# Two heads of 48 on partitions 0-47 and 64-111: attention products in parts of the TensorE array instead of zero-padded ones

## The chip, the core and the metric

The kernel runs on one core of one Trainium2 chip. A core has a matrix engine (TensorE, PE in the profile; its weight loads are PEld), a vector engine (VectorE, DVE), a scalar engine (ScalarE, ACT), GpSimd (POOL) and a queue engine (SyncE, SP) that here only issues DMAs. Each engine works through its own list of instructions in order and waits on semaphores. The metric is the device time in microseconds, lower is better. Matrix products write to PSUM, which VectorE and ScalarE read; everything else lies in SBUF, with 128 partitions.

## What is computed

A recurrent attention with a decaying state per head, then two matrix products with a squared ReLU between. Shapes: 4 batches, 8 heads, 768 tokens, head size 48; the second part has 3072 tokens, width 384, hidden width 2048. All is float32 in value (the weights of the second part come as float64).

```python
def _attn_ref(r, k, v, w, u):
    B, H, S, D = r.shape
    state = np.zeros((B, H, D, D), dtype=np.float32)
    y = np.zeros_like(r)
    for t in range(S):
        kt, vt, rt, wt = (k[:, :, t], v[:, :, t], r[:, :, t], w[:, :, t])
        cur = np.einsum('bhd,bhe->bhde', u[None] * kt, vt)
        y[:, :, t] = np.einsum('bhd,bhde->bhe', rt, state + cur)
        state = wt[:, :, :, None] * state + np.einsum('bhd,bhe->bhde', kt, vt)
    return y.astype(np.float32)

def _moe_ref(x, w_in, w_out):
    h = np.maximum(x @ w_in, 0.0)
    return (h * h @ w_out).astype(np.float32)
```

## The kernel before

Tokens are cut into 6 chunks of 128 (c), and a unit is one chunk of one batch (b), all 8 heads: 24 units. Within a chunk the recurrence becomes products of matrices: scores of the scaled keys and queries under a causal mask, their product with the values, and the product of the queries with the state before the chunk. Heads are worked on in four pairs; the 48 + 48 rows of a pair lie on partitions 0 to 95.

A unit passes through these stages:

- `load` and `load_v` (lines 129 to 141) bring w, k, r and v with tokens on partitions. v goes into a tile in which each head is followed by 48 zero columns.
- `spread` (line 143) brings w, r and k to head dimensions on partitions. In chunk 0 TensorE transposes them; later VectorE transposes blocks of 32 by 32 into z (line 160) and 12 DMAs (line 164) put the blocks into pt. It also keeps the running maximum of a test on w (`far`, line 169) and makes `beta`, the diagonal of the scores.
- `decay` (line 183): VectorE's scans over w (line 192), ScalarE's logarithm and exponential, and the scaled queries pt[:, 1] and keys pt[:, 2]. To keep a pair's heads apart in a 96-row product, zeros stand in place of the other head: in the keys in chunks 0 and 1 (Kz), and from chunk CR = 2 on in the queries, split into a leading float32r part and the rest (Rh, Rl, Kh, Kl; lines 218 to 227). Em is the decay over the chunk, laid out as a block diagonal.
- `ktok` (line 234): TensorE transposes the keys back (ktp, four products).
- `scores` (line 244), in two halves of four heads: products into mt, then a masked copy by VectorE onto M (line 257), which ScalarE has filled with beta on the diagonal (line 249). In chunks 0 and 1 four float32 products make a half; later six float32r products of 256 columns.
- `mix` (line 261): for each pair one product with the state (line 269, from chunk 1 on) and two with M and the zero-padded values (line 272) into yb. ScalarE and VectorE split yb into two float32r parts (lines 278, 279). Three pairs go straight into xT; the fourth goes through x3 and three DMAs (line 281) into xT's partitions 96 to 127.
- `state` (line 283): dS from keys and values (line 289), added to the batch's state S and scaled by Em.

The second part takes a chunk's four batches together. `moe_h` makes 128 hidden columns for 512 tokens: 9 products hp, three for each third of the width (line 307); ScalarE, VectorE and GpSimd turn them into the squared ReLU, again in two parts. `moe_o` multiplies these with w_out: 12 products ob, three for each batch (line 322). A step is one hidden block f of 16, and ob runs LAG = 3 steps behind hp. In chunk 0 the first six steps are done for two batches at a time. Weights are loaded and split into float32r parts by `load_w` and `split_w`, the first NW blocks in one pool, the others in the place of chunk 0's tiles.

The program is written in the order of a table of positions: each stage of a unit has an offset in steps (STAGES, STAGES0, lines 333 to 340), units follow each other every four steps, and everything is sorted by position. From that, the framework's scheduler sets each engine's list at build time by its own estimate of when things are ready. On the chip this list is fixed. The PSUM pool `ps_a`, two buffers of one bank, serves ktp, mt, yb and dS.

```python
    AFTER = [(decay, 2, state), (spread, 2, mix), (load_v, 2, state), (load, 2, spread)]
    ...
                x = (4 + 6 * b if c == 1 else 8 * (i - B)) + off
    ...
        at_pos(x + 0.01, half_h, c, f, bs)
        at_pos(x + n / 2 + 0.01, put, LAG)
```

A last part (from line 431) does everything again token by token if a decay was too small; with these inputs it isn't run.

Of the kernel before, what the change touches and what calls it, by code (L numbers as in the profile page):

```python
# [22 lines left out]
def kernel(  # L23
# [16 lines left out]
    C = 128  # L40
    NC = S // C
    NP = H // 2
    R = 2 * D
    NF = DF // 128
    KT = DM // 128

    NW = 11
    CR = 2
# [14 lines left out]
    far = const.tile([128, H * D], F32, name="far")  # L63
    V.memset(far, 0.0)
    nmid = const.tile([128, 1], F32, name="nmid")
    G.memset(nmid, -W_MID)
    blk = at.tile([R, 2, D], F32, name="blk")
    G.memset(blk, 1.0)
    G.affine_select(out=blk[:, 0], in_=blk[:, 0], pattern=[[0, D]], compare_op=ALU.is_ge,
                    fill=0.0, base=D - 1, channel_multiplier=-1)  # L70
    G.affine_select(out=blk[:, 1], in_=blk[:, 1], pattern=[[0, D]], compare_op=ALU.is_ge,
                    fill=0.0, base=-D, channel_multiplier=1)
# [6 lines left out]
    zero = at.tile([R, 1], F32, name="zero")  # L79
# [5 lines left out]
    decays = at.tile([R, NP, C + 1], F32, name="decays")  # L85
    V.memset(decays[:, :, 0:1], 1.0)
    Vps = [at.tile([128, H, 2, D], F32, name=f"Vp{i}") for i in range(2)]
    for t in Vps:
        V.memset(t, 0.0)
    Ss = [at.tile([R, NP, R], F32, name=f"S{b}") for b in range(B)]  # L90

    # Weights come as the bits of float64; a block of them gives way to its float32r parts, the
    # leading one and the rest, which take its place.
# [4 lines left out]
    def load_w(f):  # L98
# [5 lines left out]
        for ps, src in ((slice(0, R), w_in32[f, 0:KT * R]), (slice(R, 128), w_in32[f, KT * R:])):  # L104
            nc.sync.dma_start(out=ri[ps], in_=src.rearrange("(k p) x -> p k x", k=KT))
# [20 lines left out]
    # One unit: the C tokens of chunk c in batch b, all heads; its stages pass tiles on in `un_`.  # L126
    un_ = {}

    def load(c, b):
        ss = slice(c * C, c * C + C)  # L130
        st = ld.tile([128, 3, H * D], F32, name="st")
        for i, src in ((0, w), (2, k), (1, r)):
            nc.sync.dma_start(out=st[:, i].rearrange("s (h d) -> s h d", d=D),  # L133
                              in_=src[b, :, ss, :].rearrange("h s d -> s h d"))
        un_[c, b] = {"st": st}

    def load_v(c, b):
        ss = slice(c * C, c * C + C)
        vp = Vps[(c * B + b) % 2]
        nc.sync.dma_start(out=vp[:, :, 0], in_=v[b, :, ss, :].rearrange("h s d -> s h d"))  # L140
        un_[c, b]["vp"] = vp
# [372 lines left out]
```

## Time and profile before

| | us |
|---|---|
| median of 3 runs | 620.69 |
| lowest and highest run | 620.52, 625.94 |
| profiled execution: span of its instructions | 621.0 |
| TensorE matmuls busy | 557.3 (90%) |
| TensorE weight loads busy (beside the matmuls) | 506.8 (82%) |
| VectorE busy | 414.7 (67%) |
| ScalarE busy | 315.8 (51%) |
| GpSimd busy | 267.1 (43%) |

The profiled execution gives no other time of its own than this span.

The profile is of one execution. A row of a timeline begins with its start and its length in us, then engine, source line, operation, the tiles written and read, shape and count; in brackets the idle time of the engine ahead of it, and what ended it. Lengths of matmuls are modelled and overlap, so a rate is read from start to start. A table of stretches gives busy time and count for each engine, then the clock granted to TensorE as a share of its full speed, then the share of the DMA engines and GB/s.

### The profile page before, as it was taken

The numbers are of one execution on the slowest core, as the hardware profiler recorded it, in microseconds if no ns is written. First come the engines' busy times: TensorE is split into PE (matmuls) and PEld (weight loads), VectorE is DVE, ScalarE is ACT, GpSimd is POOL, SyncE is SP. The second block draws the span as 40 slices with busy tenths as digits, with TensorE's granted clock in tenths as the row PEclk, the third lists the DMA queues.
The fourth block names the chain that finished last, engine by engine and source line by source line (L and its number), as shares of the span: only waits on it lengthen the run. The fifth ranks groups of instructions, "written<-read, shape, count | busy, mean of one in ns | idle before, by whom it ended". The sixth has DMA issues, their size and how long they took to land.

```text
span 621.0 us, 9387 instructions
## 1 busy us (share of the span) xinstructions
PE 557.3 (90%) x3224; PEld 506.8 (82%) x3224; DVE 414.7 (67%) x639; ACT 315.8 (51%) x697; POOL 267.1 (43%) x228
## 2 busy tenths in 40 slices
PE   3476968798699998999999999999999999999994
PEld 2466958697497997988998999999989999988994
DVE  5789799887876857776967987686576765211110
ACT  3767556555565643554663655555366545242321
POOL 3364366523754534426444553353543332233230
PEclk9988779979899997999999999999999999999998
DMA  9976677257136543245445335424525230010001
GB/s 181 255 138 150 111 162 163 45 123 138 32 60 122 98 75 51 43 70 98 103 73 89 55 65 128 81 44 74 87 46 115 49 54 7 8 51 2 1 0 55
DMA packets 214212, 51.21 MB, mean 82 GB/s; under 512 B 198160, under 2 KB 212112, under 8 KB 214160
## 3 DMA queue, kind: packets, MB, share of 16 engines
q1 hardware_dynamic: 210704, 45.84, 39.5%
q10 hardware_dynamic: 3456, 4.72, 2.1%
q8 instruction: 27, 0.44, 0.3%
q14 instruction: 25, 0.20, 0.1%
HBM read 31.65 MB, written 4.72 MB: 59 GB/s over the span
## 4 chain that ended last, share of the span: by engine, by line
PE 61%; DVE 19%; DMA 5%; SPq 5%; issue 3%; POOL 3%; ACT 3%; DVEq 0%; ACTq 0%; POOLq 0%
PE hp L307 25%; PE ob L322 23%; PE yb L272 5%; PE mt L253 4%; DVE decays L192 3%; PE yb L269 2%; SPq L164 2%; DMA ri<-in_moe_w_in_dram 2%; DVE Rl L223 2%; DVE z L160 2%; SPq L133 2%; DVE q L116 2%; DVE t L311 1%; DVE pt L199 1%; DVE q L118 1%
## 5 line engine op out<-in xcount | busy, mean ns | idle before, releaser
L307 PE MATMUL hp<-xT,wi 128*128 128x512 f32 (+1 forms) x918 | 225.9, 391 | 16.2 <-DVE t L311 13.0
L314 POOL TENSOR_TENSOR g<-t,g 128x512 fp32r<-128x512 f32 (+1 forms) x102 | 134.2, 1317 | 235.6 <-ACT g L313 231.3
L322 PE MATMUL ob<-wo,g 128*128 128x384 f32 x1152 | 220.9, 340 | 0.0
L307 PEld LDWEIGHTS hp<-xT,wi 128*128 128x128 f32 x918 | 167.2, 193 | 48.5 <-DVE t L311 14.9
L322 PEld LDWEIGHTS ob<-wo,g 128*128 128x128 f32 x1152 | 201.8, 190 | 3.7
L311 DVE SCALAR_TENSOR_TENSOR t<-hp,t 128x512 f32<-128x512 f32 (+1 forms) x102 | 66.7, 654 | 123.3 <-ACT t L310 123.1
L313 ACT CAST g<-t 128x512 fp32r<-128x512 f32 (+1 forms) x102 | 60.4, 592 | 101.5 <-PE ob L322 53.6
L310 ACT ACTIVATE t<-hp 128x512 f32<-128x512 f32 (+1 forms) x102 | 57.9, 567 | 69.7 <-PE hp L307 65.8
L249 ACT ACTIVATE M<-ident,beta 128x128 f32<-128x128 f32 x192 | 64.3, 392 | 10.3 <-PE yb L272 7.2
L272 PE MATMUL yb<-M,Vp 128*96 128x128 f32 x384 | 60.0, 285 | 1.6 <-DVE M L257 1.5
L257 DVE COPY_PREDICATED M<-caus,mt 128x512 f32<-128x512 uint8 x48 | 35.2, 735 | 28.9 <-PE mt L253 22.1
L272 PEld LDWEIGHTS yb<-M,Vp 128*96 128x96 f32 x384 | 50.4, 174 | 2.2 <-DVE M L257 2.2
L173 POOL TENSOR_TENSOR st<-st 128x384 f32<-128x384 f32 x24 | 28.3, 1177 | 39.4 <-DVE z L160 38.0
L192 DVE TENSOR_TENSOR_SCAN decays<-pt,zero 96x128 f32<-96x128 f32 x80 | 41.1, 568 | 1.6 <-DMA pt<-z 1.5
L223 DVE SCALAR_TENSOR_TENSOR Rl<-pt,blk,Rh 96x512 fp32r<-96x512 f32 x32 | 34.4, 1087 | 0.2 <-ACT Rh L222 0.2
L269 PE MATMUL yb<-pt,S 96*96 96x128 f32 x160 | 31.0, 274 | 0.0
L174 POOL TENSOR_TENSOR st<-st,un 128x384 f32<-128x384 f32 x24 | 29.1, 1214 | 1.8
L160 DVE STREAM_TRANSPOSE z<-st 128x1152 f32<-128x1152 f32 x20 | 27.1, 1354 | 0.0
L240 PE MATMUL ktp<-ident,pt 96*128 96x96 f32 x80 | 11.2, 267 | 17.5 <-issue 7.9
L240 PEld LDWEIGHTS ktp<-ident,pt 96*128 96x128 f32 x80 | 9.2, 152 | 21.4 <-issue 9.1
L197 ACT ACTIVATE y<-decays 96x512 f32<-96x512 f32 x20 | 12.6, 630 | 27.0 <-DVE decays L192 26.9
L256 PE MATMUL mt<-pt,Kz 96*128 96x128 f32 x128 | 22.8, 338 | 2.7 <-DVE S L291 2.0
(79 smaller groups left out, 659.9 us busy)
## 6 DMA issues: line engine op xcount, KB each, us to landing
pt<-z SPq DMA_DIRECT2D x240, 48.0 KB, 2.1
ro<-in_moe_w_out_dram SPq DMA_DIRECT2D x16, 384.0 KB, 5.9
ri<-in_moe_w_in_dram SPq DMA_DIRECT2D x16, 288.0 KB, 5.7
st<-in_w_dram SPq DMA_DIRECT2D x24, 192.0 KB, 3.7
st<-in_k_dram SPq DMA_DIRECT2D x24, 192.0 KB, 4.1
st<-in_r_dram SPq DMA_DIRECT2D x24, 192.0 KB, 3.9
Vp<-in_v_dram SPq DMA_DIRECT2D x24, 192.0 KB, 3.5
out_dram<-os ACTq DMA_DIRECT2D x24, 192.0 KB, 1.9
```

What stands on the lines that cost most here:

```text
L160: V.transpose(out=z.rearrange("a q x i -> a x q i"), in_=st.rearrange("s t (p q x) -> s (t p) q x", q=3, x=32))
L192: V.tensor_tensor_scan(out=E[:, p, 1:C + 1], data0=wv[:, p], data1=zero.broadcast_to([R, C]), initial=1.0, op0=ALU.mult, op1=ALU.add)
L223: V.scalar_tensor_tensor(out=Rl[:, :, j], in0=Rt, scalar=blk[:, j, 0:1], in1=Rh[:, :, j].bitcast(F32), op0=ALU.mult, op1=ALU.subtract)
L249: A.activation(M[:, x], ident, AF.Copy, scale=d["beta"][:, 4 * q + x:4 * q + x + 1])
L269: T.matmul(yb[:, p], Ss[b][:, p], d["pt"][:, 1, p], start=True, stop=False)
L272: T.matmul(yb[:, p], vp[:, o:o + R], d["M", p // 2][:, 2 * (p % 2) + j], start=(c == 0 and j == 0), stop=(j == 1))
L307: T.matmul(hp, wi[f][:, wl, kt * 128:kt * 128 + 128], xT[:, kt, xl, xs], start=(m == 0), stop=(m == 3 * KT - 1))
L310: A.activation(t, hp, AF.Relu)
L311: V.scalar_tensor_tensor(out=t, in0=hp, scalar=0.0, in1=t, op0=ALU.max, op1=ALU.mult)
L313: A.copy(out=g[:, 0], in_=t)
L314: G.tensor_tensor(out=g[:, 1], in0=t, in1=g[:, 0].bitcast(F32), op=ALU.subtract)
L322: T.matmul(obs[b][:, 0:DM], g[:, gl, (b - bs[0]) * C:(b - bs[0]) * C + C], wo[f][:, wl], start=(f == 0 and n == 0), stop=(f == NF - 1 and ...
```

## The change

Each head of a pair gets 64 partitions: the even head lies on 0 to 47, the odd one on 64 to 111. Products then take one head at a time in a part of the array, by the partitions of their operands and their results:

- scores: 48 rows by 128 columns, one half of the array's rows for each head, 8 float32 products into two PSUM tiles, one per head parity. The float32r split from chunk 2 on is gone (Rh, Rl, Kh, Kl), and so are Kz and `blk`.
- yb: the state product takes a quarter of the array (48 rows, 64 or 48 columns), 8 of them instead of 4; the product with M takes half the columns, 8 as before, with values that need no zeros.
- dS: 8 products of 48 columns instead of 4 of 96, each in half of the array's columns. Em becomes the four columns Ec, and the state has 64 columns for a pair. In chunk 1 its scaling moves from VectorE to GpSimd.
- `scores` is one stage instead of two halves: all 8 products, then both masked copies.
- pt is filled by 16 DMAs for a unit (12 before), since two of the three blocks of 32 rows are cut at a head's edge or moved. xT has 112 rows by the split and 2 × 16 by DMA: 6 DMAs (3 before). w_in's first tile is loaded by 4 DMAs (2 before).
- In chunk 0 the transposes have 128 columns, of which 16 for each head are ones.
- The test on w is summed by a second pass on ScalarE (ReLU with a sum) instead of VectorE's running maximum.
- NW goes from 11 to 10.

```diff
+    J = 64
+    HP = J + D
-    NW = 11
-    CR = 2
+    NW = 10
...
+            for q, x, n, to in ((0, 0, 32, 0), (1, 0, 16, 32), (1, 16, 16, 64), (2, 0, 32, 80)):
                 for tb in range(4):
+                    nc.sync.dma_start(out=pz[to:to + n, :, 32 * tb:32 * tb + 32],
+                                      in_=z[32 * tb + x:32 * tb + x + n, q])
...
-        V.tensor_tensor(out=far, in0=w2, in1=far, op=ALU.max)
+        A.activation(w2, w2, AF.Relu, bias=nfar, accum_out=far[:, c * B + b:c * B + b + 1])
...
-    def scores(c, b, q):
+    def scores(c, b):
...
+        for p in range(NP):
+            for j in range(2):
+                js = slice(j * J, j * J + D)
+                T.matmul(mts[j][:, p], pt[js, 2, p], pt[js, 1, p], start=True, stop=True)
+        for j in range(2):
+            V.copy_predicated(out=d["M", j], mask=caus.unsqueeze(1).broadcast_to([128, NP, C]), data=mts[j])
...
+        wide = (J, D)
+        for p in range(NP) if c > 0 else ():
+            for j in range(2):
+                js = slice(j * J, j * J + D)
+                T.matmul(yb[j * J:j * J + wide[j], p], Ss[b][js, p, 0:wide[j]], d["pt"][js, 1, p],
+                         start=(p == 0), stop=False, skip_group_check=True)
         for p in range(NP):
             for j in range(2):
+                o = (2 * p + j) * D
+                T.matmul(yb[j * J:j * J + wide[j], p], d["v"][:, o:o + wide[j]], d["M", j][:, p],
+                         start=(c == 0 and p == 0), stop=True, skip_group_check=True)
...
+        n = D // KT
+        for j in range(2):
+            for q in range(KT):
+                nc.sync.dma_start(out=xT.bitcast(F32)[j * J + D:j * J + J, q, :, cs],
+                                  in_=x3.bitcast(F32)[j * J + q * n:j * J + q * n + n])
...
             for p in range(NP):
+                for j in range(2):
+                    T.matmul(dS[j * J:j * J + wide[j], p], d["Kt"][:, p, j * J:j * J + wide[j]],
+                             d["v"][:, (2 * p + j) * D:(2 * p + j) * D + D], start=True, stop=True)
...
     STAGES = [
-        (-12, load), (-4, spread), (0, load_v), (0, decay), (5, ktok),
-        (0, lambda c, b: scores(c, b, 0)), (6, lambda c, b: scores(c, b, 1)), (7, mix), (9, state),
+        (-12, load), (-4, spread), (0, load_v), (0, decay), (5, ktok), (2, scores), (7, mix), (9, state),
     ]
```

The scheduler's lists change with this. On TensorE, at the end of a chunk in the dense part, this stood before: the last products of yb of the chunk's last unit (b = 3), ob of the chunk that ends, that unit's dS, and the first hp of the new chunk, which reads xT with the columns of this unit.

```order
L272 MATMUL yb<-M,Vp_109 96x128 x2
L322 MATMUL ob_2021<-wo,g 128x384 x3
L322 MATMUL ob_2025<-wo,g 128x384 x3
L322 MATMUL ob_2029<-wo,g 128x384 x3
L322 MATMUL ob_2033<-wo,g 128x384 x3
L289 MATMUL dS<-Vp_109,Kt 96x96 x4
L322 MATMUL ob_2021<-wo,g 128x384 x3
L322 MATMUL ob_2025<-wo,g 128x384 x3
L322 MATMUL ob_2029<-wo,g 128x384 x3
L322 MATMUL ob_2033<-wo,g 128x384 x3
L322 MATMUL ob_2021<-wo,g 128x384 x2
L307 MATMUL hp<-xT,wi 128x512 x18
```

And now, at the same place on TensorE:

```order
L258 MATMUL yb<-M_2692,v_108 64x128
L258 MATMUL yb<-M_2698,v_108 48x128
L280 MATMUL dS<-v_108,Kt 64x48
L280 MATMUL dS<-v_108,Kt 48x48
L280 MATMUL dS<-v_108,Kt 64x48
L280 MATMUL dS<-v_108,Kt 48x48
L280 MATMUL dS<-v_108,Kt 64x48
L280 MATMUL dS<-v_108,Kt 48x48
L280 MATMUL dS<-v_108,Kt 64x48
L280 MATMUL dS<-v_108,Kt 48x48
L300 MATMUL hp<-xT,wi 128x512 x27
```

The 26 to 28 products of ob that stood between yb and the new chunk's hp now stand ahead of this unit's scores; dS alone is left between, and ahead of the last chunk, whose units have no dS, nothing.

On SP's queue a unit in the dense part had these rows before (transposed blocks into pt, the next loads, the fourth pair into xT):

```order
L164 DMA pt<-z 32x12x32 x12
L133 DMA st<-in_r_dram 128x8x48
L281 DMA xT<-x_1749 32x2x128 x3
L140 DMA Vp_108<-in_v_dram 128x8x48
L133 DMA st<-in_w_dram 128x8x48
```

and now:

```order
L269 DMA xT<-x_1596 16x2x128 x6
L171 DMA pt_105<-z 32x12x32 x4
L171 DMA pt_105<-z 16x12x32 x8
L171 DMA pt_105<-z 32x12x32 x4
L141 DMA st<-in_w_dram 128x8x48
```

Where 15 transfers moved a unit's blocks and its fourth pair, 22 smaller ones do now.

177 lines of the change are left out of this document (70 added, 107 removed).

## Prediction

> **What bounds the kernel now.** I read the page first, then the busy times of four stretches, then TensorE's timeline in the dense part, then the place where one chunk's products end and the next chunk's begin.
>
> The stretches (time, busy time of each engine with its count of instructions, the granted clock of TensorE, DMA):
>
> ```profile
> core 0: us, PE busy (x) PEld busy (x) DVE busy (x) ACT busy (x) POOL busy (x), PEclk, DMA share, GB/s
> 0.00:190.00 190.00, 140.89 (x834) 127.46 (x835) 158.12 (x269) 109.99 (x261) 96.37 (x96) 0.91 0.64 130
> 190.00:300.00 110.00, 104.96 (x607) 94.51 (x607) 76.86 (x112) 57.46 (x126) 45.16 (x35) 0.97 0.44 84
> 300.00:541.00 241.00, 239.77 (x1425) 220.14 (x1424) 168.44 (x244) 125.42 (x273) 104.63 (x80) 1.00 0.36 65
> 541.00:621.00 80.00, 71.67 (x363) 64.64 (x361) 11.23 (x17) 22.96 (x40) 20.90 (x18) 0.96 0.06 21
> ```
>
> There are two regimes. Up to 190 us TensorE stands idle for 49 us and VectorE is the fullest engine, 158 of 190. From 190 to 541 us TensorE is busy for 344.7 of 351 us at nearly full clock: there each microsecond put on TensorE or taken off it counts in full, and VectorE's 168 of 241 is slack. The last 80 us are products alone, which the change doesn't touch.
>
> What one unit of attention costs TensorE in the dense part is read from start to start, since the drawn lengths overlap:
>
> ```profile
> 402.52 0.28 PE L253 MATMUL mt<-Rh,Kh 96*128 96x256 f32 x1
> ...
> 403.12 0.28 PE L253 MATMUL mt<-Rh,Kl 96*128 96x256 f32 x1
> 403.23 2.25 PE L307 MATMUL hp<-xT,wi 128*128 128x512 f32 x9
> 405.33 0.38 PE L269 MATMUL yb<-pt,S 96*96 96x128 f32 x2
> ...
> 407.52 0.60 PE L272 MATMUL yb<-M,Vp 128*96 128x128 f32 x4
> 407.88 2.33 PE L322 MATMUL ob<-wo,g 128*128 128x384 f32 x12
> ...
> 412.15 0.84 PE L289 MATMUL dS<-Vp,Kt 128*96 128x96 f32 x8
> 412.77 2.33 PE L322 MATMUL ob<-wo,g 128*128 128x384 f32 x12
> ...
> 421.23 0.49 PE L240 MATMUL ktp<-ident,pt 96*128 96x96 f32 x4
> 421.50 0.36 PE L253 MATMUL mt<-Rh,Kh 96*128 96x256 f32 x1
> ```
>
> Six score products take 0.71 us (402.52 to 403.23), so a unit's twelve 1.42. The 24 records of yb take 2.55 (405.33 to 407.88), 0.106 each: a float32 product leaves two records, two passes. The 8 passes of dS take 0.62, 0.078 each at 96 columns, and ktp 0.27. A unit is 4.86 us. A step of the products is 9 hp in 2.10 and 12 ob in about 2.1 more.
>
> Where a chunk begins, its first hp reads the columns of all four batches, so the last unit's yb must have gone through ScalarE, VectorE and a DMA into xT. At 458 us that is just late:
>
> ```profile
> 451.29 0.60 PE L272 MATMUL yb<-M,Vp 128*96 128x128 f32 x4
> ...
> 453.28 0.47 ACT L278 ACTIVATE xT<-yb 96x384 fp32r<-96x384 f32 x1
> ...
> 454.43 3.02 PE L322 MATMUL ob<-wo,g 128*128 128x384 f32 x16
> 455.03 0.54 DVE L279 SCALAR_TENSOR_TENSOR xT<-yb,xT 96x384 fp32r<-96x384 f32 x1
> ...
> 455.61 0.27 ACT L278 ACTIVATE x<-yb 96x128 fp32r<-96x128 f32 x1 [0.66 <-DVE xT L279]
> ...
> 456.09 0.28 DVE L279 SCALAR_TENSOR_TENSOR x<-yb,x 96x128 fp32r<-96x128 f32 x1
> ...
> 456.40 1.86 SPq L281 DMA_DIRECT2D xT<-x  x3
> ...
> 458.36 0.93 PE L307 MATMUL hp<-xT,wi 128*128 128x512 f32 x3 [0.91 <-DMA xT<-x]
> ```
>
> From the last yb, whose four passes at 0.106 to 0.11 end at 451.7, to the first hp is 6.6 us. TensorE fills it with ob products and dS, and only 0.91 us is idle.
>
> **The change, part by part.**
>
> *Passes.* A unit now has 8 score products of two passes (16 of 128 columns), 8 yb products from the state and 8 from M (32 passes) and 8 of dS (16 passes of 48 columns). If the two heads of a pair take turns, that is 16 × 0.106 = 1.70, 32 × 0.106 = 3.39, 16 × 0.039 = 0.62, and ktp 0.27 × 112/96 = 0.32: 6.03 us, 1.17 more than 4.86. If the two parts of the array work at the same time, the first three halve: 0.85 + 1.70 + 0.31 + 0.32 = 3.18, 1.68 less. In the last chunk, without dS and ktp, it is +1.12 or −1.42. Over the 16 units from chunk 2 on (12 and 4): serial +18.5 us, paired −25.8. No row of before shows a split array. I take paired: the two heads read different partitions or write different ones, and the code issues them alternately into two banks. Both ends stay for the range.
>
> *Going between whole and split array.* A unit leaves the whole array and comes back 7 times at most (scores, state products, M products, dS), 5 where dS follows yb: 98 changes over the 16 units. What such a change costs is not in the trace either. Its bounds are 0 and a drained pipe, the drawn length of a product less its pace: 0.28 − 0.12 = 0.16 us, from the mt rows. I take the upper end, 15.7 us, since the first product after a change has nothing of its own kind ahead of it to overlap with; the lower end is 0. The Trainium skill's page "TensorEngine Tiling (Array Packing)", Key Properties, says that changing the tiling mode drains the engine; no run shown here tests it. By it the upper end holds and the sum below is 649; with no drain it would be 633.
>
> *The order at the chunk's edge.* This is the largest term; the order lists stand with the change above. Before, 28 ob products and dS stood between the last unit's yb and the next chunk's first hp. Now the ob products have all moved ahead of that unit's scores, and only dS, 0.31 to 0.62 us, is left to cover the way of yb into xT. This is so ahead of chunks 2, 3 and 4; ahead of chunk 5 there is not even dS, and ahead of chunk 1 some 32 ob products still stand there, so I count four edges. The way itself grows: on SP's queue the two heads' rows go out in six transfers instead of three, and the first hp needs the fourth of them. An issue on SP takes, and a transfer lands after (minimum/median/maximum, ns, then us):
>
> ```profile
> L281 SPq DMA_DIRECT2D xT<-x x72: 585/594/1521, 36.8 to 540.0; - x72
> ...
> DMA to landing us min/median/max: 1.8/1.9/4.5
> ```
>
> The wait at an edge: the four passes over yb are 0.47 + 0.54 + 0.27 + 0.28 = 1.56 us, three issues ahead of the fourth 1.8, the landing 1.9, less 0.31 for dS: 5.0 at least. With all the queueing of before it is 6.6 + 1.8 − 0.31 = 8.1. ScalarE and VectorE lose work just there (below), so I take 6.2, near the middle. In front of yb stands a smaller wait: both masked copies of the scores now follow the last score product, 0.75 us each on VectorE, with only 3 ob products between (0.52): 0.5 us. Then the clock:
>
> ```profile
> 164.70:171.50 6.80, 4.98 (x13) 4.11 (x14) 6.80 (x10) 3.28 (x7) 4.12 (x3) 0.50 0.00 0
> ...
> 239.80:246.60 6.80, 6.33 (x23) 5.85 (x22) 3.28 (x6) 1.92 (x5) 1.28 (x1) 0.50 0.34 57
> ```
>
> ```profile
> 166.52 4.21 PE L307 MATMUL hp<-xT,wi 128*128 128x512 f32 x9 [6.07 <-DVE t L311]
> 239.44 0.55 PE L240 MATMUL ktp<-ident,pt 96*128 96x96 f32 x4 [2.46 <-issue]
> ```
>
> After idle times of 6.07 and 2.46 us the clock was 0.50 for 6.8 us, of which TensorE was busy for 4.98 and 6.33: half of that, 2.5 and 3.2 us, is lost. I add 2.8 at each edge. An edge costs 0.5 + 6.2 + 2.8 = 9.5, four of them 38 us. Ends: 4 × 5.0 = 20 with no clock loss and no copy wait, and 4 × (8.1 + 3.2 + 0.9) = 49.
>
> The third unit of each chunk has 4 products of 0.2 us between its scores and yb, 0.3 short of the copies: 1 us in all.
>
> *VectorE, ScalarE, POOL.* From chunk 2 on a unit loses Rl twice, Kl and the running maximum; the squares' test becomes a second pass on ScalarE, which loses Rh and Kh. All of this lies beside a busy TensorE and is worth nothing there, except the shorter queues used above. Em's product becomes a copy of four columns; the state's product in chunk 1 goes from VectorE to POOL. POOL was busy for 267 of 621 us, so it covers that.
>
> *The start.* Here VectorE counts:
>
> ```profile
> L169 DVE TENSOR_TENSOR far<-w,far 128x384 f32<-128x384 f32 x10 | 7.6, 756 | 2.8 <-ACT w L168 2.8
> L294 DVE TENSOR_TENSOR S<-S,Em 96x384 f32<-96x384 f32 x4 | 2.2, 546 | 0.0
> ```
>
> ```profile
> 66.07 8.47 SPq L164 DMA_DIRECT2D pt<-z  x12
> ...
> 79.02 1.36 DVE L192 TENSOR_TENSOR_SCAN decays<-pt,zero 96x128 f32<-96x128 f32 x4
> ...
> 187.25 2.96 PE L307 MATMUL hp<-xT,wi 128*128 128x512 f32 x12
> ```
>
> The last row is chunk 1's first products, at 187 us. 9.8 us leave VectorE by 190 us. Against that SP, which had the transposed tiles of chunk 1's first unit issued only at 74.5, four microseconds before the scans, issues 16 transfers instead of 12 (8.47 × 4/12 = 2.8) and three more of xT (1.8): 4.6 us later for each of four units, all on VectorE's path at most. The extra weight issues queue in the same place. Bounds: −9.8 and +18.4. I take half of VectorE's gain and one unit's delay, which cancel to about −1: only that first unit is seen waiting on SP. The paired products of chunks 0 and 1 fall into TensorE's idle time and count nothing.
>
> **Sum:** 621.0 − 25.8 + 15.7 + 38 + 1 − 1 = 649 us. The profiled execution's span of 621.0 stands 0.3 above the median of the runs, 620.69; I add nothing for it.
>
> **The rivals.**
>
> *The column halves do not pair.* The M products of yb and dS use all 128 rows twice, with two moving operands from the same partitions; if these must take turns, yb's M part costs 1.70 instead of 0.85 and dS 0.62 instead of 0.31: 1.16 more in 12 units, 0.85 in 4, 17.3 us: 666. For it: nothing in the trace shows two streams at once. Against it: whole-array passes follow at full pace, so streaming and not loading limits them. The Trainium skill's page "TensorE: Matmul & The Clock Gate", Part 3, says that a weight load overlaps a running matmul only where the row group differs, which would tell against column halves in the same way. The trace does not bear this out for the whole array, with 220.14 us of loads in 241 us beside 239.77 us of matmuls.
>
> *Nothing pairs.* The change then doesn't do what it says: +18.5 for −25.8: 693. Against it speaks only that the code keeps rows, columns and banks apart.
>
> *The start is what decides, and the kernel is faster.* If VectorE's in-order queue is what holds TensorE back up to 190 us, 9.8 us off it can end several of the waits, and each clock window of 2.8 us behind them. The most it can give is the idle 49 us: 600. It decides from 34 us on (649 to 615); at 40 us it gives 609. For it: VectorE busy 158 of 190. Against: SP gets 4.6 us more per unit in the same stretch.
>
> **How the numbers follow.** Paired with the edges: 0.41, 649, by itself from 625 (edges at 20, changes of mode at 8) to 665. Column halves in turn: 0.18, 666. Nothing pairs: 0.12, 693. The start decides: 0.19, 609. Gains and losses cancel within 1%, for instance with edges at 20 and no price for mode changes (621 − 25.8 + 20 + 1 − 1 = 615): 0.10. The predicted time is 649. A range from 606 to 688 leaves out about half of the faster case, 0.10, and most of the serial one, 0.09. Of this kernel about 1%, 6.2 us, can be told from no change: faster 0.19 and a little of the cancelling case, 0.21; slower the paired case and the two serial ones, 0.69; same 0.10.
>
> **What would show it.** In the profile of the changed kernel: yb's 32 passes start to start in some 1.7 us (paired), 2.6 (column halves in turn) or 3.4 us (serial); score products in 0.85 or 1.7. Idle time of about 6 us before hp, put down to DMA xT<-x, at four chunk edges, and a clock of 0.50 behind each. Chunk 1's first hp within 10 us of 187. The prediction is wrong if the edges are idle for under 3 us, if chunk 1 begins before 155 us, or if units take TensorE less than 2.5 us.

## The result and the profile after

The kernel after the change takes 688.62 us (median of 4 runs, 687.47 to 690.39), the kernel before beside it 621.29 (620.52 to 625.94). The ratio is 1.1072, 95% interval 1.102 to 1.1124. The forecast was slower, 649 us, and 606 to 688: the direction holds, the time lies just above the range, and the move is +67 us instead of +28. The profiled execution of after has a span of 686.2 us, 65.2 above the 621.0 of before, and the comparison below is made between these two.

Both executions, cut where each chunk's first hp starts (time, busy time and count of each engine, granted clock, DMA share, GB/s; the rows are the start, chunks 1 to 4, and the last products). Before:

```profile
0.00:187.30 187.30, 138.19 (x823) 125.27 (x824) 155.42 (x267) 109.20 (x259) 94.03 (x95) 0.91 0.64 130
187.30:280.60 93.30, 88.35 (x508) 79.45 (x507) 66.43 (x95) 48.30 (x106) 38.86 (x31) 0.96 0.41 75
280.60:369.70 89.10, 88.68 (x532) 80.96 (x531) 69.44 (x93) 46.84 (x104) 44.58 (x34) 1.00 0.44 81
369.70:458.40 88.70, 87.79 (x530) 80.45 (x528) 64.09 (x96) 48.70 (x106) 41.64 (x34) 1.00 0.42 77
458.40:541.00 82.60, 82.60 (x477) 75.99 (x478) 48.04 (x75) 39.83 (x84) 27.04 (x21) 1.00 0.26 49
541.00:621.00 80.00, 71.67 (x363) 64.64 (x361) 11.23 (x17) 22.96 (x40) 20.90 (x18) 0.96 0.06 21
```

And after, with the stretch of half clock around one chunk edge and around the last:

```profile
0.00:208.20 208.20, 143.39 (x919) 121.06 (x919) 138.19 (x253) 103.20 (x253) 92.72 (x100) 0.80 0.59 116
208.20:310.50 102.30, 91.27 (x608) 79.14 (x609) 44.63 (x77) 43.38 (x100) 33.87 (x32) 0.93 0.38 66
310.50:413.10 102.60, 91.38 (x609) 79.31 (x609) 44.49 (x77) 43.46 (x100) 33.90 (x32) 0.93 0.38 66
413.10:515.60 102.50, 91.26 (x608) 79.13 (x609) 44.90 (x77) 43.47 (x100) 33.16 (x31) 0.93 0.38 66
515.60:607.50 91.90, 84.20 (x529) 73.16 (x529) 38.18 (x65) 35.93 (x80) 29.34 (x22) 0.96 0.31 55
607.50:686.20 78.70, 70.37 (x338) 62.66 (x338) 11.23 (x17) 22.91 (x40) 20.83 (x17) 0.93 0.06 22
...
404.60:418.30 13.70, 5.21 (x12) 4.13 (x13) 6.17 (x11) 2.85 (x6) 3.06 (x3) 0.50 0.56 95
606.00:612.80 6.80, 5.30 (x13) 4.22 (x14) 0.40 (x1) 0.60 (x1) 0.00 (x0) 0.50 0.05 10
```

Length less PE busy is idle time: in the four chunk stretches 11.0, 11.2, 11.2 and 7.7 us, 41.2 in all, against 5.0, 0.4, 0.9 and 0, 6.3 before. Half of the busy time in a window of clock 0.50 is lost. Such a window follows the first hp of each of the chunks 1 to 4, some 2.6 us each and 10.5 in all, against 3.2 before (the window that the prediction shows at 239.8); the one behind the last edge, at 607.5 us, falls into the last stretch. What is left, the products at full clock, is 347.7 us against 344.3. So the 65.2 us lie in three places: 20.9 in the start, 35 of idle time and 7 of lost clock in the chunk stretches, and 3.4 in the products, less 1.3 at the end. The 3.4 are no price of the split products: the chunk stretches now hold 768 records of ob where they held 747, the last stretch 192 where it held 217, and as 12 take about 2.1 us, 21 are 3.7. Counted so, the products of attention cost the same as before. VectorE lost 93 us of work (414.7 to 321.6) and no stretch became shorter by it.

The waits of TensorE from 200 us on (instruction, what it waited for, us in total, times, longest) say where the idle time is:

```profile
PE hp L300 <- DMA xT<-x: 39.0, 4, 11.2
```

The edge at 413 us, from the timeline of after:

```profile
395.70 11.00 SPq L171 DMA_DIRECT2D pt<-z  x16
...
400.43 1.09 PE L258 MATMUL yb<-M,v 128*64 128x128 f32 x16
401.35 0.62 PE L280 MATMUL dS<-v,Kt 128*48 128x48 f32 x16
...
403.40 0.29 DVE L265 SCALAR_TENSOR_TENSOR x<-yb,x 112x128 fp32r<-112x128 f32 x1 [0.47 <-ACT x L264]
...
408.03 0.90 SPq L141 DMA_DIRECT2D st<-in_r_dram  x1
409.02 3.84 SPq L269 DMA_DIRECT2D xT<-x  x6
...
413.09 1.19 PE L300 MATMUL hp<-xT,wi 128*128 128x512 f32 x2 [11.12 <-DMA xT<-x]
```

The rows for xT are ready on VectorE at 403.7 us and leave SP at 409.0. SP isn't idle: it issues the next unit's 16 tile transfers until 406.7 and then three loads. These 5.3 us account for the difference between the 6.2 that the prediction took for the way from yb to hp and the 11 that are seen. At 607 us, ahead of the last chunk, there is no next unit, and the same wait is 5.75.

A unit of the dense part of after, on TensorE:

```profile
421.82 0.55 PE L221 MATMUL ktp<-ident,pt 112*128 112x112 f32 x4
422.30 2.01 PE L237 MATMUL mt<-pt 48*128 48x128 f32 x16
424.24 2.35 PE L300 MATMUL hp<-xT,wi 128*128 128x512 f32 x9
426.52 1.08 PE L253 MATMUL yb<-pt,S 48*64 48x128 f32 x16
427.53 1.09 PE L258 MATMUL yb<-M,v 128*64 128x128 f32 x16
428.55 2.37 PE L315 MATMUL ob<-wo,g 128*128 128x384 f32 x12
...
432.95 0.67 PE L280 MATMUL dS<-v,Kt 128*64 128x48 f32 x16
433.55 2.37 PE L315 MATMUL ob<-wo,g 128*128 128x384 f32 x12
```

The scores of a unit of the last chunk, which has no ktp:

```profile
524.38 1.16 PE L237 MATMUL mt<-pt 48*128 48x128 f32 x16
525.47 2.36 PE L300 MATMUL hp<-xT,wi 128*128 128x512 f32 x9
```

From start to start the unit of chunk 4 above takes: ktp 0.48, scores 1.94, yb 2.03, dS 0.60, 5.05 us in all against 4.86 before. yb's 32 passes in 2.03 overlap (taken apart, below, they need 3.0). The scores do and don't. In the last chunk their 16 passes take 1.09 us, two at a time (in two of its units, whose first passes are further apart, 1.40 and 1.49). In the 12 units before it they take 1.78 to 1.94, nearly all one after another at 0.11 us, where a pass through the whole array took 0.106 before.

The difference is in the order that the scheduler builds for TensorE, which doesn't keep the program's alternation. With A for a product of the even head and B for one of the odd head, a unit's eight products stand as A A A A B B B B in the first unit of the chunks 2 to 4 and as A A A B B B A B in their other units; in the last chunk they stand as A B A B A B A B. In the units with ktp, A's tile and ktp hold the two buffers of `ps_a`, and B's tile needs one of them: the first B starts 0.05 us after ScalarE has copied ktp out (at 341.57 us behind a copy that ends at 341.52). That the scheduler puts A's products first for this reason is argued; no run changes the pool.

The start: before, xT of chunk 0's last batch left SP at 76.29 us, and the second half of chunk 0's first layer began at 80.57.

```profile
76.29 1.87 SPq L281 DMA_DIRECT2D xT<-x  x3
...
80.57 0.59 PE L307 MATMUL hp<-xT,wi 128*128 128x256 f32 x3 [1.56 <-DVE decays L192]
```

After, the same transfer stands behind 16 tile transfers and a weight block of five, and the second half stands behind chunk 1's first ktp and scores in TensorE's list:

```profile
71.59 10.74 SPq L171 DMA_DIRECT2D pt<-z  x16
...
84.16 1.37 DVE L199 TENSOR_TENSOR_SCAN decays<-pt,zero 112x128 f32<-112x128 f32 x4 [4.82 <-DMA pt<-z]
...
84.98 3.77 SPq L269 DMA_DIRECT2D xT<-x  x6
...
88.20 0.69 PE L315 MATMUL ob<-wo,g 128*128 128x384 f32 x1 [8.33 <-ACT g L306]
...
95.86 1.65 PE L315 MATMUL ob<-wo,g 128*128 128x384 f32 x4 [4.52 <-POOL g L307]
...
98.18 2.76 PE L237 MATMUL mt<-pt 48*128 48x128 f32 x16
...
100.87 0.58 PE L300 MATMUL hp<-xT,wi 128*128 128x256 f32 x1
```

That is 20.3 us late at 101 us, and 20.9 at chunk 1's first hp. xT is not what ended last here: its last transfer left SP at 88.75 us and a landing takes about 2. Ahead of the second half, TensorE's list has six ob, which wait for ScalarE's and GpSimd's squares; these stand behind work on the scans of chunk 1's first unit, and VectorE began these scans only when the 16 tile transfers had landed. The first hp is late too, at 58.35 us instead of 51.30: in the list it now stands behind the third batch's yb and dS, which came after it before. So the first theory for all that follows: it is the transfers on SP, whose in-order queue holds xT and the tiles back, and not the products, that cost the time.

### The profile page after: what moved, and what is told of

Same layout as the page of the kernel before. It is cut to its first block, busy times and chain, and to the rows that moved or that the text cites. A ratio compares the mean times of both kernels' runs of the same rounds, so it can differ in the third digit from the quotient of the medians.

```text
span 686.2 us, 10287 instructions
## 1 busy us (share of the span) xinstructions
PE 571.9 (83%) x3608; PEld 494.5 (72%) x3608; DVE 321.6 (47%) x562; ACT 292.4 (43%) x673; POOL 243.8 (36%) x234
## 4 chain that ended last, share of the span: by engine, by line
PE 70%; SPq 8%; DVE 6%; DMA 5%; issue 4%; POOL 4%; ACT 1%; DVEq 0%; ACTq 0%; POOLq 0%
PE hp L300 28%; PE ob L315 27%; SPq L171 6%; PE mt L237 6%; PE yb L258 3%; PE yb L253 3%; PE ktp L221 2%; DVE decays L199 1%; PE dS L280 1%; SPq L269 1%; DMA pt<-z 1%; POOL g L307 1%; DMA xT<-x 1%; DMA v<-in_v_dram 1%; DVE M L239 1%
## 5 line engine op out<-in xcount | busy, mean ns | idle before, releaser
L300 PE MATMUL hp<-xT,wi 128*128 128x512 f32 (+1 forms) x918 | 239.7, 410 | 59.8 <-DMA xT<-x 39.0
L237 PE MATMUL mt<-pt 48*128 48x128 f32 x384 | 50.1, 321 | 2.8 <-ACT Kt L223 1.2
L237 PEld LDWEIGHTS mt<-pt 48*128 48x128 f32 x384 | 44.3, 216 | 8.4 <-issue 2.1
L199 DVE TENSOR_TENSOR_SCAN decays<-pt,zero 112x128 f32<-112x128 f32 x80 | 32.3, 465 | 25.2 <-DMA pt<-z 25.2
L258 PE MATMUL yb<-M,v 128*64 128x128 f32 (+1 forms) x384 | 29.6, 303 | 3.8 <-DMA v<-in_v_dram 2.9
L129 POOL TENSOR_TENSOR wi<-q,wi 128x384 fp32r<-128x384 f32 x16 | 17.8, 1119 | 35.8 <-ACT wi L128 25.2
L258 PEld LDWEIGHTS yb<-M,v 128*64 128x64 f32 (+1 forms) x384 | 23.4, 144 | 8.8 <-issue 3.9
L181 DVE TENSOR_REDUCE beta<-st 128x8 f32<-128x384 f32 x24 | 13.2, 551 | 27.1 <-POOL st L180 27.0
L204 ACT ACTIVATE y<-decays 112x512 f32<-112x512 f32 x20 | 12.6, 629 | 30.5 <-DVE decays L199 30.5
L207 DVE TENSOR_TENSOR pt<-decays,y 112x512 f32<-112x512 f32 x20 | 17.6, 878 | 15.0 <-ACT y L205 15.0
```

Source lines behind the costliest of these rows:

```text
L199: V.tensor_tensor_scan(out=E[:, p, 1:C + 1], data0=wv[:, p], data1=zero.broadcast_to([HP, C]), initial=1.0, op0=ALU.mult, op1=ALU.add)
L237: T.matmul(mts[j][:, p], pt[js, 2, p], pt[js, 1, p], start=True, stop=True)
L258: T.matmul(yb[j * J:j * J + wide[j], p], d["v"][:, o:o + wide[j]], d["M", j][:, p], start=(c == 0 and p == 0), stop=True, skip_group_check ...
L300: T.matmul(hp, wi[f][:, wl, kt * 128:kt * 128 + 128], xT[:, kt, xl, xs], start=(m == 0), stop=(m == 3 * KT - 1))
```

## The experiments

Times are medians. "Before" in the same jobs was 619.4 to 620.7 us.

### The tiles' transfers on two queues

```diff
-                    nc.sync.dma_start(out=pz[to:to + n, :, 32 * tb:32 * tb + 32],
+                    (nc.sync, nc.scalar)[tb % 2].dma_start(out=pz[to:to + n, :, 32 * tb:32 * tb + 32],
```

> The changed kernel with every second of the 16 transfers into pt issued from ScalarE's queue instead of SP's. In the built order some 36 ob products then stand between the last unit's yb and the next chunk's hp again. Theory (the edges cost 45 to 50 us of the 67, and come from SP being too slow for a unit, in the order as on the chip): edges idle under 1 us, chunks 2 to 4 take 87 to 90 us instead of 102.5, time 635 to 648. Rival (the split products themselves make the dense part slower): edges vanish, but chunks take over 93 us, time over 655.

Measured: 639.33 us, ratio 1.0269 (1.022 to 1.0318), 49 us less than after. The edge at 392 us:

```profile
387.48 4.30 PE L315 MATMUL ob<-wo,g 128*128 128x384 f32 x23
...
388.60 3.77 SPq L269 DMA_DIRECT2D xT<-x  x6
...
392.48 1.86 PE L300 MATMUL hp<-xT,wi 128*128 128x512 f32 x7 [0.70 <-DMA xT<-x]
```

xT leaves SP as soon as it is ready (388.6), and the list that the scheduler builds has ob products behind yb again. That this is so because its estimate of a unit's pace no longer hangs on 16 issues of one queue is argued, not shown. The idle time in the chunk stretches falls from 41.2 to 3.8 us. The first three take 92.7, 91.2 and 92.5 us, more than the theory's 87 to 90, in an execution of 645.3 us, 6 above the median. The start stays: chunk 1 begins at 208.6.

With GpSimd's queue in place of ScalarE's (`(nc.sync, nc.gpsimd)[tb % 2]`):

> As e2_pt_two_queues, but the odd transfers of the transposed tiles go out on GpSimd's queue instead of ScalarE's. Theory (what counts at the edges is that SP is free for xT, whichever queue takes the other half): edges under 2 us idle, chunks 2 to 4 of 91 to 94 us, time 634 to 645. Rival (GpSimd, in order behind products of 1.3 us, sends its half late and the scans wait): chunks over 97 us, time over 655.

Measured: 638.73 us, ratio 1.0291 (1.0237 to 1.0345). The edges wait for xT for 0.5 us in all: which queue takes the other half made no difference that these runs show. Chunk 1 begins at 209.9.

### xT on another queue, the tiles left on SP

```diff
-                nc.sync.dma_start(out=xT.bitcast(F32)[j * J + D:j * J + J, q, :, cs],
+                nc.scalar.dma_start(out=xT.bitcast(F32)[j * J + D:j * J + J, q, :, cs],
```

> The changed kernel with the six transfers of yb's fourth pair into xT issued from ScalarE's queue; TensorE's order at the chunk edges stays (all ob ahead of the last unit). Theory: of the 11.1 us idle at an edge, some 5.3 us are xT's transfers queued on SP behind 16 pt transfers and 3 loads, and some 1.2 us more come from the slower issues; so the edges fall to 4 to 6 us, the half-clock windows behind them from 13.7 to 6.8 us, and the time by 4 x 5 to 7 = 20 to 28 us, to 660 to 669. Rival (the way of yb through ScalarE and VectorE and the landing make the wait): edges of 9 to 11 us, time within 5 us of 688.6.

Measured: 741.72 us, ratio 1.1932 (1.1889 to 1.1976). The edges went as the theory has it (5.8, 6.0, 5.7 and 5.7 us idle), and the time went up by 53. Chunk 1 begins at 223.2, 15 us later, and from there on ktp waits in ten units, 19.3 us in all. On GpSimd's queue (`nc.gpsimd`):

> The kernel after the change, with the six transfers of xT on GpSimd's queue and all else on SP as it was. Theory (SP's in-order queue holds xT back behind other transfers, at the edges and in chunk 0 alike, where xT of the last batch left SP at 85.0 us behind 16 tile transfers and a weight block, against 76.3 before the change): the second half of chunk 0's hp begins before 92 us instead of 100.9, chunk 1 at 192 to 202 instead of 208.2; the edges, whose ob products are still drained ahead, idle 5 to 7 us instead of 11; time 655 to 668. Rival for the start (VectorE's and ScalarE's own order of work sets it): chunk 1 at 206 to 211, the edges alone gain, 668 to 676.

Measured: 713.12 us, ratio 1.1441 (1.1356 to 1.1526). The second half of chunk 0 began at 83.8 us and chunk 1 at 199.0, both as expected, and the edges fell, to 27.3 us for the four together; the time missed by 45 us. Of TensorE's waits from 200 us on in e9_xt_gpsimd one is new:

```profile
PE ktp L221 <- issue: 14.1, 9, 3.0
```

In nine units ktp stands too early in TensorE's list and waits for its own unit's last product on VectorE (at 438.12 us it starts 0.1 us after it), and behind five of these waits, of 1.1 to 3.0 us, a window of half clock begins within 3 us. So the lists change with a change to the queues, and a shorter queue isn't a gain by itself.

### The scores in quarters of the array

```diff
-                T.matmul(mts[j][:, p], pt[js, 2, p], pt[js, 1, p], start=True, stop=True)
+                for h in range(2):
+                    hs = slice(h * J, h * J + J)
+                    T.matmul(mts[j][hs, p], pt[js, 2, p, hs], pt[js, 1, p], start=True, stop=True)
```

> The changed kernel with the scores multiplied in quarters of the array: keys 0 to 63 and 64 to 127 of a chunk apart, 16 products instead of 8. Theory: the two row halves take turns because each pass loads 128 columns of weights in about 109 ns and loads into the same columns follow one another; with 64 columns the four quarters work at once, and the scores' 16 passes of 1.78 us become 32 passes in 0.9 to 1.0 us. Rival (two row halves cannot work at once, whatever is loaded): 32 passes in pairs, 1.7 to 1.8 us. Time: 0.85 us less in 16 units of the dense part, 0 to 14 us off 688.6, since the edges stay; by the rival within 3 us.

Measured: 681.61 us, ratio 1.0978 (1.0945 to 1.1011). In the units with ktp the 32 quarter passes take 1.71 to 1.87 us from start to start where the 16 row-half passes took 1.78 to 1.94, and in the last chunk 1.04 to 1.49 where those took 1.09 to 1.49. Theory and rival both miss the reason: row halves with 128 columns do run at once, where the list alternates them. Where one head's products stand together, its column quarters pair, and twice the passes take the same time. The passes save 0.07 us in each of 12 units, 1 us in all; the time fell by 7.0, and where the other 6 come from isn't shown (the profiled execution, of 688.2 us, isn't one of the faster ones). Together with the two queues:

> e2_pt_two_queues and e3_scores_quarters together. Theory (the two add: the quarters gave 7 us in e3, most of it as 32 passes in 1.5 to 1.7 us instead of 16 in 1.78, which now stand on a TensorE that never idles): 630 to 636. Rival (e3's 7 us came from its edges and its start, and the passes themselves give 16 units times 0.15 = 2.4 us): 636 to 639.

Measured: 632.09 us, ratio 1.018 (1.0134 to 1.0227): the two add up, and this is the fastest of the changed kernels. Its chunk stretches sum to 350.2 us where those of before sum to 353.7; what it loses is the start alone, 202.9 against 187.3. TensorE is busy for 349.1 of the 350.2 us, and was for 347.4 of the 353.7: what the stretches gained is idle time and lost clock, and not shorter products.

### The pairs taken apart

The same split products, but in yb and dS first all of one head's half, then all of the other's (with e2_pt_two_queues' transfers):

```diff
-        for p in range(NP):
-            for j in range(2):
+        for j in range(2):
+            for p in range(NP):
```

> e2_pt_two_queues with the same split products in another order: in yb and dS all products of the first head's half, then all of the second's. Theory (only products that stand next to each other and lie in different halves run at once): yb takes 32 passes one after another, 3.4 to 3.6 us instead of 2.0, dS 0.6 to 0.9; some 1.6 to 1.9 us a unit, 16 units, so 26 to 30 us on a TensorE that doesn't idle there: 662 to 672 against 639.3. Rival (TensorE pairs them in any order, or the pairs gave nothing): 636 to 645.

Measured: 663.0 us, ratio 1.0665 (1.0607 to 1.0722), 23.7 us over e2_pt_two_queues.

```profile
421.66 1.56 PE L253 MATMUL yb<-pt,S 48*64 48x128 f32 x16
423.16 1.57 PE L258 MATMUL yb<-M,v 128*64 128x128 f32 x16
```

The 16 passes of the state take 1.50 us from start to start instead of 1.01. The column halves, which read the same rows, pair as the quarters do: M's part of yb takes 1.49 here and took 1.02 in after. yb as a whole takes 2.99, less than the theory's 3.4 to 3.6, and dS 0.76 instead of 0.60. Over the units this comes to some 17 us; the other 6 or 7 aren't accounted for.

### The start

Six kernels test where the start's 21 us come from. The narrow weight pieces on ScalarE's queue (`nc.scalar.dma_start(out=ri[j * J + D:j * J + J], in_=last)`):

> The changed kernel with the 32 small transfers of w_in (16 partitions each) issued from ScalarE's queue, so that SP has two for a block as before the change. Theory (the start lost 21 us to SP's longer queue, of it the weights' issues a third): chunk 1's first products at 195 to 203 us instead of 208, time 676 to 684. Rival (the start is lost to something else, such as the order of the first units): 206 to 212 us, time within 4 us of 688.6.

Measured: 689.57 us, ratio 1.1112 (1.1072 to 1.1151), chunk 1 at 209.0: no effect. The weights' ring 11 deep again (`NW = 11`), with the tiles on two queues:

> The tiles' transfers on two queues as in e2_pt_two_queues, and the ring of early weights again 11 blocks deep, as before the change (it was cut to 10). Theory (of the 21 us that the start lost, a good part is waiting for the eleventh weight block, since hp waits 9.4 us on the casts of the weights in the start): chunk 1 begins at 195 to 203 instead of 208.6, time 627 to 634 against 639.3. Rival (the start is lost in the order of the units' own work, not in the weights): chunk 1 again at 207 to 210, time 637 to 641.

Measured: 647.71 us, ratio 1.0438 (1.0387 to 1.049), chunk 1 at 212.9: not the ring, both theories were too low. The scores of chunk 0 at their old offset (`(5.0, scores)` for `(1.5, scores)`):

> As e2_pt_two_queues, but in chunk 0 the score products are called at the place of before (offset 5.0, so behind the unit's other work, instead of 1.5, which the list's order makes 2.5). Theory (moving the scores forward puts the M fills and masked copies of the next units ahead of the split of the first units' outputs, so the first hp came 7 us late at 58.4 and more followed): first hp back near 51, chunk 1 begins at 195 to 203, time 627 to 634. Rival: the first hp moves but the stretch up to chunk 1 is held elsewhere: chunk 1 at 206 to 210, time 637 to 641.

Measured: 634.86 us, ratio 1.0261 (1.0209 to 1.0313), not told apart from e2_pt_two_queues by these runs; chunk 1 at 200.1, but the first hp again at 58.8, so not for the theory's reason. And beside the quarters, in e14_pt2_quarters_offset:

> e8_pt2_quarters and e6_pt2_old_offset together: transfers on two queues, scores in quarters, chunk 0's scores called at the place of before. Theory (the start keeps its loss, since xT stays behind other transfers on SP): chunk 1 at 198 to 204, time 627 to 634, not under the kernel before. Rival (the two savings in the start add to e8's): chunk 1 at 188 to 196, time 617 to 625.

Measured: 633.05 us, ratio 1.0199 (1.0158 to 1.024), chunk 1 at 203.4: the theory's numbers. Then xT on GpSimd's queue, with tiles on two queues and quarters:

> e8_pt2_quarters with xT on GpSimd's queue; nothing else differs from it. Theory (xT waiting on SP is the start's loss): second half of chunk 0's hp before 92 us instead of 97, chunk 1 at 188 to 198 instead of 202.9, time 617 to 626. Rival: chunk 1 at 201 to 206, time 629 to 636.

Measured: 633.32 us, ratio 1.0251 (1.0196 to 1.0307). Its timeline in the start:

```profile
79.26 1.89 DVE L199 TENSOR_TENSOR_SCAN decays<-pt,zero 112x128 f32<-112x128 f32 x3 [2.61 <-DMA pt<-z]
79.48 1.71 PE L302 MATMUL hp<-xT,wi 128*128 128x256 f32 x13
```

The first hp is at 52.1 us and the second half of chunk 0 follows the first without a gap, at 80.6, both as before the change. So with xT off SP the start's loss up to 81 us is gone. That xT's own wait was the loss isn't shown by this, since more than that wait changed: the first hp stands ahead of the third batch's yb and dS again, as before the change, and the tiles, no longer behind xT on SP, come earlier, so that the scans begin at 79.3 us instead of 83.9 in e8_pt2_quarters. And chunk 1 begins at 195.2, 8 us late, and the total doesn't fall, as the stretch of chunk 1 takes 94.3 us instead of 90.4. The gain is given back further on, and why isn't settled. Last, all of the weights' transfers on GpSimd's queue:

> e8_pt2_quarters with the five transfers of each weight block on GpSimd's queue; nothing else differs from it. Theory (it is the sum of SP's issues in the start that holds back xT, the loads and the tiles; a weight block takes five of them, some 2.2 us, where it took three): chunk 1 at 188 to 198 instead of 202.9, time 617 to 626. Rival (the weights come in time for nothing better, or GpSimd's busy queue sends them late): chunk 1 at 201 to 215, time 629 to 645.

Measured: 650.46 us, ratio 1.052 (1.0466 to 1.0574): TensorE stands idle for 19.4 us, until 37.8, for the load of a unit, and chunk 1 begins at 214.5. The rival holds.

### The old products with the new transfers

The kernel before, its products untouched, with its transfers cut as the change cuts them:

```diff
-            for q in range(3):
+            for q, x, n in ((0, 0, 32), (1, 0, 16), (1, 16, 16), (2, 0, 32)):
...
-        for q in range(KT):
+        for j in range(2):
+            for q in range(KT):
...
-            nc.sync.dma_start(out=ri[ps], in_=src.rearrange("(k p) x -> p k x", k=KT))
+            nc.sync.dma_start(out=ri[ps.start:ps.start + h], in_=src[0:h])
+            nc.sync.dma_start(out=ri[ps.start + h:ps.stop], in_=src[h:])
```

> The kernel before the change, its products untouched; only its transfers on SP are cut up as the change cuts them: 16 instead of 12 for the transposed tiles of a unit, six instead of three for xT, five instead of three for a weight block. Theory (the loss at the edges and in the start comes from the count of SP's issues, directly and through the order that is built from it, and not from the split products): edges at chunks 2 to 4 idle 4 to 11 us where before they idled under 1, chunk 1 at 195 to 210 instead of 187.3, time 650 to 685. Rival (the split products and their longer way through the engines make the loss): edges under 3 us, chunk 1 within 5 us of 187, time 619 to 632.

Measured: 702.85 us, ratio 1.1332 (1.1287 to 1.1377): slower than the whole change. Its edge at 415 us:

```profile
398.14 10.89 SPq L167 DMA_DIRECT2D pt<-z  x16
...
405.21 1.30 PE L327 MATMUL ob<-wo,g 128*128 128x384 f32 x6
...
406.34 0.29 DVE L282 SCALAR_TENSOR_TENSOR x<-yb,x 96x128 fp32r<-96x128 f32 x1
...
410.42 4.04 SPq L285 DMA_DIRECT2D xT<-x  x6
...
414.69 1.62 PE L312 MATMUL hp<-xT,wi 128*128 128x512 f32 x3 [8.17 <-DMA xT<-x]
```

At the edge it is the picture of after with the old products: ob drained ahead (6 left), xT ready at 406.6 and sent at 410.4, 8 us idle. The four edges wait 29.1 us for xT; another 14.5 are waits of ktp in nine units, which after doesn't have. Chunk 1 begins at 198.1. The transfers alone, with the lists that follow from them, cost 82 us, and the whole change is 14 faster than this; by which of its parts isn't shown. One part at a time:

> The kernel before the change with only the transposed tiles' transfers cut up, 16 instead of 12 for a unit; xT in three and weight blocks in three as they were. Theory (the four extra issues of the tiles are what makes the edges: with them the planned order leaves 7 ob products instead of 35 behind the last unit's yb, and SP is busy with the next unit's tiles when xT is due): edges idle 5 to 8 us, chunk 1 within 6 us of 187, 650 to 680. Rival (xT's six issues and the weights' make most of it): 620 to 640.

Measured: 677.16 us, ratio 1.0913 (1.0872 to 1.0954), as the theory has it in time; chunk 1 begins at 193.7, 6.4 us late. The chunk stretches idle 8 to 11 us each, at an edge in two pieces (2.6 us ahead of the first hp at 396.5, another 2.6 ahead of an hp at 405.1, which waits for VectorE), and 11.4 us of it are waits of ktp in nine units.

> The kernel before the change with only xT's transfers cut up, six instead of three; tiles in 12 and weight blocks in three as they were. Theory (the order at the edges keeps its 35 ob products behind yb, so three issues of 0.6 us hide there; in chunk 0 they delay the first products by some 2 us a unit): edges under 3 us, chunk 1 at 188 to 195, 620 to 634. Rival (xT's six issues alone bring the edges back, as the prediction's own working of the edge put them first): over 640.

Measured: 660.48 us, ratio 1.0661 (1.0621 to 1.0701). The theory missed, and so did the rival's reason. Chunk 1 begins at 185.3, earlier than before. The largest of TensorE's waits from 186 to 580 us:

```profile
PE ktp L240 <- issue: 14.8, 6, 2.9
```

No edge waits for xT. Six units' ktp wait, as in e9_xt_gpsimd. One unit shows what moved; before the change VectorE's scans and the unit's ktp stood so:

```profile
318.28 1.04 DVE L192 TENSOR_TENSOR_SCAN decays<-pt,zero 96x128 f32<-96x128 f32 x3
...
332.69 0.49 PE L240 MATMUL ktp<-ident,pt 96*128 96x96 f32 x4
```

and the same unit here:

```profile
309.75 7.89 SPq L164 DMA_DIRECT2D pt<-z  x12
...
328.70 2.13 DVE L192 TENSOR_TENSOR_SCAN decays<-pt,zero 96x128 f32<-96x128 f32 x4
...
338.41 0.52 PE L240 MATMUL ktp<-ident,pt 96*128 96x96 f32 x4 [2.44 <-issue]
```

TensorE's order around ktp is as before. But the scans now come behind the earlier unit's yb and state on VectorE, 9.7 us ahead of ktp where they came 14.4 ahead, though SP had issued their last tile at 317.6. So it isn't the queue that makes them late but VectorE's list. With three issues of 0.6 us more in a unit, the built lists changed so that 40 us were lost, while SP issued for only 13 of a unit's some 25 us (22 transfers of 0.6). So the number of transfers works in two ways, by the queue on the chip and by the order that is planned from it. How the loss of after divides between the two isn't settled, since no run changed the one without the other.

## Why the prediction was right and wrong

**Passes and mode changes**, −25.8 + 15.7 = −10.1 predicted, about 0 measured (+3.4, less the 3.7 of moved ob products). yb was to take 1.70 and two changes of 0.16, 2.02: measured 2.03. dS 0.31 and two changes, 0.63: 0.60. The scores were to take 0.85 and two changes, 1.17: measured 1.09 in the best units of the last chunk, but 1.78 to 1.94 in the 12 units with ktp, 0.61 to 0.77 more, some 8 us. Pairing itself was right, for quarters, column halves and row halves. The step that failed is its reason, "the code issues them alternately into two banks": the program does, but in those 12 units TensorE's list has most of one head's scores first and then the other's, and products of the same half don't pair. The rival "the column halves do not pair" is refuted by 1.02 for M's 16 passes. The Trainium skill's page "TensorEngine Tiling (Array Packing)", Key Properties, says that different tiles run in parallel; the trace agrees, with 1.01, 1.02 and 1.09 us for 16 passes in quarters, column halves and row halves. It also says that a change of mode drains the engine. The sums of yb and dS agree with 0.16 us for each change, but no run here tells such a drain from a slower pace of the pairs.

**The chunk's edge**, +38 and +1 predicted, 35 + 7 = 42 measured, in the place and with the releaser that were named, and with the clock at 0.50 behind. The size is nearly right by a balance. The idle time was to be 27 us and grew by 35: three edges wait 11 us instead of 6.2, because xT stands behind the next unit's tiles on SP, which the working of the edge left out (it counted xT's own issues); the copy wait of 0.5 an edge came to 1.4 in all, and the last edge waited 5.75. The lost clock was to be 11 us and grew by 7 only, as the 3.2 of before went away.

**The start**, −1 predicted, +20.9 measured: the largest miss. The step that failed is "I take half of VectorE's gain and one unit's delay, which cancel": 17 us less work on VectorE up to chunk 1 (155.4 to 138.2) gave nothing. The first hp came 7 us late, put behind the third batch's work by the planned order. The second half of chunk 0 came 20.3 late, behind ob products that hang, through VectorE's scans, on 16 tile transfers of one queue, and behind chunk 1's scores. The price of an issue on SP was right (0.6 us); what was missing was the question which work stands behind which. Cut transfers alone move chunk 1 to 198.1 (e12_before_split_dmas), about half of it; the rest is open.

**VectorE, ScalarE and POOL** off the path in the dense part: right. **The rivals:** "nothing pairs", 693, lies near the measured time by luck, and its reason is refuted by e13_pt2_unpaired, where taking the pairs apart costs 23.7 us. "The start decides, and the kernel is faster" was right in that the start weighs much, and wrong in its sign, as less work on VectorE didn't shorten it.

**The lists.** The prediction saw in the order that ob had moved ahead of the last unit and took it as given by the change of products. The runs show that it follows from the tiles' transfers on SP: 16 with the old products move ob ahead (e12_before_split_dmas, and e15_before_tiles16 with nothing else changed), six for xT don't (e16_before_xt6), and 16 on two queues with the new products leave it behind yb (e2_pt_two_queues).

## What to carry to other kernels

Before a layout is changed for the sake of TensorE, count the transfers that the new partitions cut in two, for each queue, and read in the timeline which late transfer will stand behind them: here 22 instead of 15 in a unit, with the lists built for them, cost more than the array's halves could give. When a scheduler builds the lists from its own estimate, a transfer more is also a change of order, so price it by building both and comparing the lists, of every engine, at each place where an engine waits. Moving transfers to another queue must be measured: half of the tiles' saved 49 us, and xT's six cost 53 on ScalarE's queue and 24 on GpSimd's. Split products paired only where products of different parts stood next to each other in the list that the engine got, so this list must be read too, and not the program's order. A result tile that has to wait for a PSUM buffer is a place to look.

## What the runs showed of the hardware

Float32 products in different parts of the array ran at once when they stood next to each other: 16 passes took 1.01 us in quarters, 1.02 in column halves and 1.09 in row halves with 128 columns. Taken apart, the quarters took 1.50, and the row halves, where one head's mostly stood together, 1.78. The Trainium skill's page "DMA: Bandwidth & Descriptors", "Issuing engines are not separate DMA queues", says that issuing from several engines saves only the sequencer's time, usually small beside the transfer. Here this time counted: an issue on SP takes 0.6 us beside a landing of about 2, and 16 of them held xT back at each edge; taking half of these to another queue saved 49 us, the order built for it included. At the edge of 413 us TensorE stopped at 402.0, the clock stood at 0.50 from 404.6 to 418.3, and 5.2 us of products ran in that window.
